# A fused retention and FFN kernel on one core: units of 256 tokens cut in chunks of 64 instead of 128 from block 2 on

## The chip, the cores and the metric

The kernel runs on 1 core of one Trainium2 chip. The metric is the device time of one execution in microseconds (us). The times before are the median of 3 runs. The trace is of one profiled execution, which was timed as well.

In this text PE is TensorE's matmul, PEld its weight load, DVE is VectorE, ACT ScalarE, POOL GpSimd, and SP the engine whose queue issues most of the DMAs.

## The reference

Four sequences (`batch`) with 8 heads of 768 tokens and head size 64 go through a linear recurrence with a decay of its own for each head. Its result, as 3072 tokens of 512 features, goes through two dense layers with a PReLU between.

```python
gamma = 1.0 - 2.0 ** (-5.0 - np.arange(H))
for t in range(S):
    state = gamma * state + einsum('bhd,bhe->bhde', k[:, :, t], v[:, :, t])
    y[:, :, t] = scale * einsum('bhd,bhde->bhe', q[:, :, t], state)
x = y.transpose(0, 2, 1, 3).reshape(B * S, H * D)      # 3072 x 512
h = x @ w_in                                           # 512 -> 2048
out = (maximum(h, 0) + alpha * minimum(h, 0)) @ w_out  # 2048 -> 512
```

## The kernel before, in words

**Tiles, units, blocks.** The recurrence is computed in chunks. A unit `u` is 256 tokens of one sequence: three units to a sequence (`NUS`), twelve in all. A unit has two tiles `w = 2u + g`, 24 in all. Tile `g` holds 256 tokens by 4 heads; a partition holds two neighbouring tokens `a` (token 2p + a), so that its two halves of 64 partitions are the two chunks `c` of 128 tokens. Two units are a block `n` of 512 tokens, six in all, and each block goes through `ffn1` (L540) and `ffn2` (L570).

**The way of a tile.** `load` (L145) has SP issue three DMAs of 256 KB for k, q and v; each partition takes four runs of 512 B. `prep` (L183) scales k and q by powers of the decay into `kdq`, float16 (`scaled`, L190, one instruction each, on POOL from tile 8 on), transposes `kdq` into `kq` so that the head dimension lies on the partitions (from tile 8, `NPE`, on by a DMA transpose from SP at L204, before by PE in `turn`, L230), and casts v into `vx` (L211). The powers are taken relative to the end of a chunk of 128 tokens, so that a state is multiplied by the decay to the 128th at the end of each chunk.

**The products.** Per unit there are four kinds, all on 64 by 64 quadrants of PE, so that four run side by side (`DIAG`, L253):
- scores, k against q within a chunk, masked by DVE into `m2`;
- sums, k against v, the new part of the state;
- inner products, `m2` against `vx`, into `y`;
- carried products, the state at a chunk's start against q, added into `y`; those whose row half equals the chunk are issued first, the others only when a small instruction of DVE or ACT has told that the first are through (`through`, L370), since both write one bank.

The order of the work on each engine is the order of the program: the schedule is written out by hand. In blocks 0 and 1 single tiles go through `visit`, `within` and `finish`. From unit 4 on `both(u_old, u_new)` (L425) does the inner and carried products of one unit and the scores and sums of the next in one call. Before, its order on PE is: the scores of the second new tile, half of them into an `f` bank named `low` and half beside the sums; inner products of both old tiles; carried products of the same half; the scores of the first new tile into the pair of banks `s`; the sums; the carried products of the other half. `masks` (L446) multiplies scores by the causal mask in three parts. DVE then adds the carried state to the sums (L511) and multiplies by the decay (L513) for each of the two chunks. ACT copies `y` to `xT`, the input of `ffn1` (L498).

**The blocks.** The loop at L754 runs `ffn1(n)` and `ffn2(n)` as generators of 64 matmuls each of 512 columns; `tick(gen, m)` issues m of them. `ffn1` sends each of its 16 results through ACT and DVE (L537, L526); `order` names the PSUM bank that each takes. Inside `ffn2(n)` the calls of `both` for the next block are placed: in block 1 after 8 ticks (only scores and sums of unit 4), 28 more and 21 more; in the later blocks after 20 and 33 more. `ahead` (L746) prepares the next tile `w` and then loads tile `w + 4`. So SP's queue holds, in order, the loads of tiles 8 to 11, four stores of block 0's output, then for each tile its transpose followed by the three loads of the tile four on; the stores of each block's output (L602) stand in the same queue.

Of the kernel before, what the change touches and what calls it, by code (L numbers as in the profile page):

```python
# [18 lines left out]
def kernel(  # L19
# [14 lines left out]

    nc = tc.nc
# [24 lines left out]
    for g in range(2):  # L60
        for x in range(2):
            for r in range(2):
                tab_np[64 * r : 64 * r + 64, 32 + 2 * g + x] = g64[4 * g + 2 * r + x] ** 128
    ALT = 48
# [8 lines left out]
    mi_np[:, 256:384] = np.eye(128)  # L73

# [9 lines left out]
    mask = mi[:, 0:256]  # L84
    ident = mi[:, 256:384]
# [59 lines left out]
    def load(w, which="kqv"):  # L145
        u, g, b, c3 = place(w)
        t = staged.setdefault(w, {})
        for nm in which:
            src = {"k": k, "q": q, "v": v}[nm]
            t[nm] = sbp.tile([128, 4, 2 * D], FP, tag=f"{nm}s", bufs=8, name=f"{nm}s{w}")  # L150
            nc.sync.dma_start(  # L151
                out=t[nm],
                in_=src[b, 4 * g : 4 * g + 4, TU * c3 : TU * c3 + TU, :].rearrange(
                    "h (p a) d -> p h (a d)", a=2
                ),
            )
# [26 lines left out]
    def prep(w, opening=False, k_on=None, q_on=None):  # L183
        u, g, b, c3 = place(w)
        t = staged.pop(w)
        kdq = sbp.tile([128, 2, 4, 2, D], F16, tag="kdq", bufs=8, name=f"kdq{w}")
        vx = sbp.tile([128, 4, 2, D], F16, tag="vx", bufs=8, name=f"vx{w}")
        kq = sbp.tile([128, 8, 128], F16, tag="kq", bufs=8, name=f"kq{w}")

        def scaled(eng, kind, src):  # L190
            eng.tensor_tensor(  # L191
                out=kdq[:, kind].rearrange("p z r d -> p r z d"),
                in0=src.rearrange("p (r x) (a d) -> p r (x a) d", a=2, x=2),
                in1=tab[:, 16 * kind + 8 * g : 16 * kind + 8 * g + 8]
                .rearrange("p (r z) -> p r z", r=2)
                .unsqueeze(3)
                .to_broadcast([128, 2, 4, D]),
                op=MULT,
            )

        scaled(k_on or (nc.vector if opening else nc.gpsimd), 0, t["k"])
        scaled(q_on or nc.gpsimd, 1, t["q"])
        if w >= NPE:
            nc.sync.dma_start_transpose(  # L204
                out=kq, in_=kdq.rearrange("p k z r d -> p (k z r d)")
            )
        v_in = t["v"].rearrange("p h (a d) -> p h a d", a=2)
        if opening:
            v_ins[w] = vx, v_in
        else:  # L210
            nc.gpsimd.tensor_copy(out=vx, in_=v_in)  # L211
        prepped[w] = (kdq, kq, vx)
# [86 lines left out]

    def masked(w):  # L300
        kdq, kq, vx, sc = live[w]
        m2 = sbp.tile([128, 4, 2, 128], F16, tag="m2", bufs=4, name="m2")
        nc.vector.tensor_tensor(  # L303
            out=m2.rearrange("p s a i -> p s (a i)"),
            in0=sc.rearrange("p (s n) -> p s n", n=256),
            in1=mask.unsqueeze(1).to_broadcast([128, 4, 256]),
            op=MULT,
        )
        live[w][3] = m2

    def new_state():
        return sbp.tile([128, 4, D], F16, tag="tg", bufs=8, name="tg")

    def state(w, cs=None):
        u, g, b, c3 = place(w)
        decay = tab[:, 32 + 2 * g : 34 + 2 * g].unsqueeze(2).to_broadcast([128, 2, D])
        for c in cs or chunks(w):
# [4 lines left out]
            if 2 * u + c + 1 not in tgs:  # L322
                tgs[2 * u + c + 1] = new_state()
            nc.vector.tensor_tensor(out=tgs[2 * u + c + 1][:, gs], in0=stv, in1=decay, op=MULT)

    def single(g, c, r):
        return slice(256 + 256 * c + 128 * r, 384 + 256 * c + 128 * r)

    def double(g, c, r):
        return slice(512 * c + 256 * g + 128 * r, 512 * c + 256 * g + 128 * r + 128)  # L330

    def carried(w, y, started, same, after=None, at=single):
        u, g, b, c3 = place(w)
        kq = live[w][1]
        for x in range(2):
            for r in range(2):
                c = r if same else 1 - r
                if c3 + c == 0:
                    continue
                ins = nc.tensor.matmul(  # L340
                    out=y[half(x), at(g, c, r)],
# [12 lines left out]
    def inner(w, y, started, at=single):  # L354
        u, g, b, c3 = place(w)
        vx, m2 = live[w][2:4]
        for r in range(2):
            for a in range(2):
                for c, x in DIAG:
                    nc.tensor.matmul(  # L360
                        out=y[half(x), at(g, c, r)],
# [63 lines left out]
    def both(u_old, u_new):  # L425
# [6 lines left out]
        def score(w, at):  # L432
            kq = prepped[w][1]
            for x in range(2):
                for a in range(2):
                    for r, c in DIAG:
                        last = nc.tensor.matmul(  # L437
                            out=at[r][x][half(c), 128 * a : 128 * a + 128],
                            lhsT=kq[half(r), 2 * x + a, half(c)],
                            rhs=kq[half(r), 4 + 2 * x : 6 + 2 * x, half(c)],  # L440
                            start=True,
                            stop=True,
                        )
            return last

        def masks(dst, src):  # L446
            nc.vector.tensor_tensor(  # L447
                out=dst.rearrange("p s a i -> p s (a i)"),
                in0=src.rearrange("p (s n) -> p s n", n=256),
                in1=mask.unsqueeze(1).to_broadcast([128, dst.shape[1], 256]),  # L450
                op=MULT,
            )

        if new:
            u, _, b, c3 = place(new[0])
            cs = chunks(new[0])
            low = ps("low", "fb" if flip["f"] else "fa")
            sums = [ps(f"sums{c}", "pa" if c == 0 else "pb") for c in range(2)]
            beside = [t[:, 256:512] for t in sums]
            there = through(score(new[1], ((low[:, 0:256], low[:, 256:512]), beside)))  # L460
            m2 = [sbp.tile([128, 4, 2, 128], F16, tag="m2", bufs=4, name="m2") for _ in new]
            masks(m2[1][:, 0:2], low)
        if old:
            y = ps("y", "y")
            started = set()
            for w in old:
                inner(w, y, started, double)
            for w in old:
                last = carried(w, y, started, True, None, double)
            done = through(last, nc.scalar)  # L470
        if new:
            sc = ps("sc", "s")
            score(new[0], [[sc[:, 512 * r + 256 * x :][:, 0:256] for x in range(2)] for r in range(2)])
            for w in new:
                kdq, kq, vx = prepped[w]
                for x in range(2):
                    for a in range(2):
                        for c, r in DIAG:
                            if c in cs:
                                at = 128 * (w % 2) + 64 * x  # L480
                                ins = nc.tensor.matmul(  # L481
                                    out=sums[c][half(r), at : at + 64],
                                    lhsT=kdq[half(c), 0, 2 * x + a, r, :],
                                    rhs=vx[half(c), 2 * r + x, a, :],
                                    start=(a == 0),
                                    stop=(a == 1),
                                )
                                if there is not None:
                                    behind(ins, there, "the other row half wrote this bank")
                                    there = None  # L490
        if old:
            for w in old:
                carried(w, y, started, False, done if w == old[0] else None, double)
                live.pop(w)
            n, i = divmod(u_old, 2)
            if i == 0:
                xT[n] = new_x(n)
            nc.scalar.activation(  # L498
                out=xT[n][:, 4 * i : 4 * i + 4].rearrange("p c r (i a) -> p (c r) i a", a=2),
                in_=y.rearrange("p (s a i) -> p s i a", a=2, i=64),  # L500
# [4 lines left out]
        if new:  # L505
            for c in range(2):
                masks(m2[1][:, 2 + c : 3 + c], beside[c])
            for c in cs:
                stv = sums[c][:, 0:256].rearrange("p (z e) -> p z e", e=D)
                if c3 + c > 0:  # L510
                    nc.vector.tensor_tensor(out=stv, in0=tgs[2 * u + c], in1=stv, op=ADD)  # L511
                tgs[2 * u + c + 1] = new_state()
                nc.vector.tensor_tensor(  # L513
                    out=tgs[2 * u + c + 1],
                    in0=stv,
                    in1=tab[:, 32:36].unsqueeze(2).to_broadcast([128, 4, D]),
                    op=MULT,
                )
            masks(m2[0], sc)
            for w, m in zip(new, m2):  # L520
                live[w] = [*prepped.pop(w), m]
# [232 lines left out]
    for n in range(1, NBLK):  # L754
        gen = ffn1(n, "fyfpsYpS" if n > 1 else "spyfSpYf")
# [7 lines left out]
        if n + 1 < NBLK:  # L763
            tick(gen, 8)
            if n == 1:
                both(None, u0)
            ahead()
            ahead()
            tick(gen, 28 if n == 1 else 12)
            both(u0, u0 + 1)  # L770
            tick(gen, 21 if n == 1 else 33)
# [33 lines left out]
```

## Time and profile before

| What | Value |
|---|---|
| Median of 3 runs | 210.43 us (209.54 to 210.77) |
| The profiled execution's own time | 211.09 us |
| Its span, first to last instruction | 209.1 us |
| Mean granted TensorE clock | 0.998 |
| `ffn2` matmuls (L582), 400 | 87.2 us busy |
| `ffn1` matmuls (L557), 392 | 84.8 us busy |
| DMA, mean over the span | 183 GB/s, 38.27 MB |
| Loads of k, q, v | 72, 256 KB each |

The shares of busy time are of the span. Matmuls are pipelined, so their busy times overlap, and the times of the products are better read from the chain of waits, which follows the work that ended last and gives each piece only the time that it added. A DMA share can stand a little over 1, since the time of a packet includes what it overlaps with its neighbours. In a row of the stretches the columns are: the stretch, its length, then for each engine busy time and number of instructions, the granted clock, the DMA share and GB/s.

### The profile page before, as it was taken

Reading aid. Unit: us, or ns where it says so; the run is one execution under the profiler, and the core shown is the slowest. Engines: PE = TensorE matmul, PEld = TensorE weight load, DVE = VectorE, ACT = ScalarE, POOL = GpSimd, SP = SyncE. Lnnn points to the kernel's source line nnn. Section 1 sums busy time; section 2 is a strip of 40 time slices with the busy share of each in tenths; the row PEclk is TensorE's granted clock in tenths of the full one; section 3 lists DMA queues with packets and bytes.
Section 4 is the critical chain, followed back from the end, with each engine's and each line's share of the span. In section 5 each row is a group of like instructions: output and inputs, shape, how many; then the busy total and the mean of one; then the engine's idle time right before and its main releaser. Section 6 shows DMA issues by size and latency. Waiting matters only on the chain.

```text
span 209.1 us, 5197 instructions
## 1 busy us (share of the span) xinstructions
PE 201.5 (96%) x2135; PEld 101.5 (49%) x2135; DVE 123.2 (59%) x209; ACT 97.9 (47%) x166; POOL 72.8 (35%) x97
## 2 busy tenths in 40 slices
PE   7988999999999999999999999999999999999993
PEld 2565445445444555444555444545444544444452
DVE  2583886557588834888373688354888340588000
ACT  2572865174666122666233566233566123665121
POOL 0388798479927664345450054000000000000000
PEclk9999999999999999999999999999999999999999
DMA  6999999999999999799911399111410111100112
GB/s 179 307 286 345 389 389 383 371 312 306 358 254 253 298 252 202 248 233 265 266 71 74 104 235 211 53 56 56 122 31 0 50 53 50 53 0 0 50 55 96
DMA packets 64119, 38.27 MB, mean 183 GB/s; under 512 B 19152, under 2 KB 57568, under 8 KB 64096
## 3 DMA queue, kind: packets, MB, share of 16 engines
q1 hardware_dynamic: 63632, 37.69, 64.6%
q8 instruction: 16, 0.26, 0.5%
q10 hardware_dynamic: 464, 0.25, 0.5%
q14 instruction: 7, 0.06, 0.1%
HBM read 27.45 MB, written 6.29 MB: 161 GB/s over the span
## 4 chain that ended last, share of the span: by engine, by line
PE 88%; SPq 4%; DMA 3%; DVE 1%; ACT 1%; issue 1%; POOL 0%; DVEq 0%; ACTq 0%
PE hps L557 40%; PE ops L582 39%; SPq L151 4%; DMA wi<-in_moe_w_in_dram 3%; PE y L360 2%; PE y L340 2%; PE low L437 1%; PE sums L481 1%; PE sc L437 1%; PE trb L239 1%; DVE m L303 1%; ACT kq L245 0%; PE sc L267 0%; ACT os L596 0%; PE st L292 0%
## 5 line engine op out<-in xcount | busy, mean ns | idle before, releaser
L582 PE MATMUL ops<-wout,gt 128*128 128x512 f16 (+1 forms) x400 | 87.2, 371 | 0.3 <-ACT os L596 0.3
L526 DVE SCALAR_TENSOR_TENSOR gt<-hm,oma,hps 128x512 f16<-128x512 f32 x96 | 71.2, 747 | 26.4 <-ACT hm L537 16.7
L557 PE MATMUL hps<-xT,win 128*128 128x512 f16 (+1 forms) x392 | 84.8, 375 | 0.5 <-POOL win L181 0.5
L537 ACT ACTIVATE hm<-hps 128x512 f32<-128x512 f32 x96 | 57.0, 597 | 24.9 <-PE hps L557 24.5
L557 PEld LDWEIGHTS <-win 128*128 128x128 f16 x392 | 38.0, 98 | 45.3 <-POOL win L181 0.7
L582 PEld LDWEIGHTS <-gt 128*128 128x128 f16 x400 | 37.9, 98 | 41.4 <-issue 0.6
L596 ACT ACTIVATE os<-ops 128x512 f32<-128x512 f32 (+2 forms) x25 | 14.2, 576 | 46.6 <-PE ops L582 46.6
L191 POOL TENSOR_TENSOR kdq<-ks,tab 128x512 f16<-128x512 f32 x19 | 19.8, 1042 | 38.6 <-DMA ks<-in_k_dram 30.5
L191 POOL TENSOR_TENSOR kdq<-qs,tab 128x512 f16<-128x512 f32 x22 | 23.2, 1054 | 9.4 <-DMA ks<-in_k_dram 7.8
L447 DVE TENSOR_TENSOR m<-low,mi 128x512 f16<-128x512 f32 x8 | 5.5, 686 | 24.8 <-issue 24.0
L245 ACT ACTIVATE kq<-trb 128x512 f16<-128x512 f16 (+1 forms) x12 | 8.6, 736 | 10.7 <-PE trb L239 10.6
L211 POOL CAST vx<-vs 128x512 f16<-128x512 f32 x16 | 9.8, 610 | 3.5 <-PE y L360 3.0
L181 POOL CAST win<-wi 128x512 f16<-128x512 f32 x16 | 9.8, 613 | 2.8 <-DMA wi<-in_moe_w_in_dram 2.3
L181 POOL CAST wout<-wo 128x512 f16<-128x512 f32 x16 | 9.6, 613 | 3.3 <-DMA wo<-in_moe_w_out_dram 3.1
L303 DVE TENSOR_TENSOR m<-sc,mi 128x1024 f16<-128x1024 f32 x8 | 9.8, 1222 | 0.8 <-PE sc L267 0.4
L498 ACT ACTIVATE xT<-y 128x1024 f16<-128x1024 f32 x8 | 8.2, 1023 | 3.3 <-PE y L340 3.3
L447 DVE TENSOR_TENSOR m<-sc,mi 128x1024 f16<-128x1024 f32 x8 | 9.7, 1214 | 0.0
L340 PE MATMUL y<-kq,tg 64*64 64x128 f16 x160 | 8.5, 224 | 0.5 <-ACT word L374 0.4
L360 PE MATMUL y<-m,vx 64*64 64x128 f16 x384 | 8.3, 218 | 0.2 <-DVE m L303 0.2
L219 PE MATMUL trb<-ones 128*128 128x512 f16 (+1 forms) x21 | 6.5, 434 | 1.5 <-DVE word L624 1.4
L374 ACT ACTIVATE word<-word 1x1 f32<-1x1 f32 x11 | 2.2, 201 | 12.1 <-PE y L340 12.1
L600 DVE COPY os<-ops 128x128 f32<-128x128 f32 x1 | 0.3, 291 | 12.8 <-ACT os L596 12.8
(39 smaller groups left out, 99.5 us busy)
## 6 DMA issues: line engine op xcount, KB each, us to landing
ks<-in_k_dram SPq DMA_DIRECT2D x24, 256.0 KB, 4.6
qs<-in_q_dram SPq DMA_DIRECT2D x24, 256.0 KB, 4.7
vs<-in_v_dram SPq DMA_DIRECT2D x24, 256.0 KB, 4.8
out_dram<-os SPq DMA_DIRECT2D x23, 256.0 KB, 2.2
wi<-in_moe_w_in_dram SPq DMA_DIRECT2D x16, 256.0 KB, 6.1
wo<-in_moe_w_out_dram SPq DMA_DIRECT2D x16, 256.0 KB, 5.3
kq<-kdq SPq DMA_TRANSPOSE x16, 4.9
mi<-mi_const ACTq DMA_DIRECT2D x1, 128.0 KB, 3.5
```

What stands on the lines that cost most here:

```text
L181: nc.gpsimd.tensor_copy(out=dst, in_=t)
L191: eng.tensor_tensor(out=kdq[:, kind].rearrange("p z r d -> p r z d"), in0=src.rearrange("p (r x) (a d) -> p r (x a) d", a=2, x=2), in1=tab ...
L211: nc.gpsimd.tensor_copy(out=vx, in_=v_in)
L303: nc.vector.tensor_tensor(out=m2.rearrange("p s a i -> p s (a i)"), in0=sc.rearrange("p (s n) -> p s n", n=256), in1=mask.unsqueeze(1).to_ ...
L340: ins = nc.tensor.matmul(out=y[half(x), at(g, c, r)], lhsT=tgs[2 * u + c][half(r), 2 * g + x, :], rhs=kq[half(r), 4 + 2 * x : 6 + 2 * x, h ...
L360: nc.tensor.matmul(out=y[half(x), at(g, c, r)], lhsT=vx[half(c), 2 * r + x, a, :], rhs=m2[half(c), 2 * r + x, a, :], start=(c, x) not in s ...
L447: nc.vector.tensor_tensor(out=dst.rearrange("p s a i -> p s (a i)"), in0=src.rearrange("p (s n) -> p s n", n=256), in1=mask.unsqueeze(1).t ...
L526: nc.vector.scalar_tensor_tensor(out=gt[:, ft, lo:hi], in0=hm, scalar=oma_sb[:, ft : ft + 1], in1=hps, op0=MULT, op1=ADD,)
L537: nc.scalar.activation(out=hm, in_=hps, func=RELU, bias=0.0, scale=-1.0)
L557: nc.tensor.matmul(out=hpss[ft][:, 128 * lo : 128 * hi], lhsT=w_in_all[:, hp, 128 * ft : 128 * ft + 128], rhs=xT[n].rearrange("p (g t) r i ...
L582: nc.tensor.matmul(out=opss[tq], lhsT=gt[:, ft, 128 * tq : 128 * tq + 128], rhs=w_out_all[:, ft, at], start=(ft == 0), stop=(ft == NFT - 1),)
L596: nc.scalar.activation(out=os_sb, in_=opss[tq][:, cut], func=COPY, bias=0.0, scale=1.0)
```

## The change

From unit 4 (block 2's first, tile 8) on a tile is 128 tokens by all 8 heads, one token to a partition, and its two chunks are 64 tokens each. A unit of 256 tokens is again two tiles, now one after the other in time.

- `load`: a partition takes eight runs of 256 B, one of each head, where it took four of 512 B.
- `scaled`: two instructions of half the size each, with tables of their own.
- Scores, inner products and carried products have 64 columns instead of 128. A unit has 32 scores (32 before), 32 inner products (32), 32 sums (32), 32 carried products (16). In a sequence's last unit the sums of the last chunk are left out as before.
- All scores go into the pair `s`, and one mask instruction of 1024 columns serves the unit. The parts in `low` and beside the sums go, and with them one tell by DVE.
- The state is stepped four times per unit. The powers stay relative to the end of 128 tokens, so between the two chunks of a tile the sums are only added, and the decay is multiplied in at the end of a tile.
- In `both` the old unit's inner and carried products come first, then the scores and sums of the new one, then the other carried products.
- Buffers: `m2` 3 instead of 4, states 12 instead of 8. The bank order of `ffn1` changes from block 2 on.
- Places: in `ffn2` both `ahead` calls come first. In block 1 `both` comes after 2 ticks, 24 and 26 more; in the later blocks after 14 and 28 more.

Shortened to its core:

```diff
 def load
+            else:
+                at = TU * c3 + 128 * g
+                nc.sync.dma_start(
+                    out=t[nm].rearrange("p a (b d) -> p (a b) d", b=2),
+                    in_=src[b, :, at : at + 128, :].rearrange("h p d -> p h d"),
+                )
...
 def both
+        if old:
+            for w in old:
+                                out=out_of(y, w, x, c, g, r),
+                                lhsT=vx[half(c), 2 * g + r, x, :],
+                                rhs=m2[half(c), at : at + 64],
+            for w in old:
+                last = carry(w, y, True)
+            done = through(last, nc.scalar)
         if new:
+            js = range(3 if c3 == NUS - 1 else 4)
             sc = ps("sc", "s")
+            for w in new:
+                            out=sc[half(c), at : at + 64],
+                            lhsT=kq[half(r), z, half(c)],
+                            rhs=kq[half(r), 4 + z, half(c)],
+            for w in new:
+                                out=sums[c][half(r), at : at + 64],
+                                lhsT=kdq[half(c), 0, z, r, :],
+                                rhs=vx[half(c), 2 * (z // 2) + r, z % 2, :],
         if old:
+                carry(w, y, False, done if w == old[0] else None)
...
+            for j in js:
+                t, c = divmod(j, 2)
+                    nc.vector.tensor_tensor(out=stv if last else to, in0=tgs[4 * u + j], in1=stv, op=ADD)
+                if last:
+                    nc.vector.tensor_tensor(out=to, in0=stv, in1=tab[:, 32:36]..., op=MULT)
...
-        gen = ffn1(n, "fyfpsYpS" if n > 1 else "spyfSpYf")
+        gen = ffn1(n, "fspyfSpY" if n > 1 else "spyfSpYf")
...
-            tick(gen, 8)
+            ahead()
+            ahead()
+            tick(gen, 2 if n == 1 else 14)
             if n == 1:
                 both(None, u0)
-            ahead()
-            ahead()
-            tick(gen, 28 if n == 1 else 12)
+                tick(gen, 24)
             both(u0, u0 + 1)
-            tick(gen, 21 if n == 1 else 33)
+            tick(gen, 26 if n == 1 else 28)
             both(u0 + 1, u0 + 2 if 2 * u0 + 4 < NW else None)
```

## Prediction, before the change was run

> **What bounds the kernel now.** I read the page's shares first, then the chain of waits around the attention steps of the FFN blocks, then the queue that loads q, k and v.
>
> ```profile
> PE 201.5 (96%) x2135; PEld 101.5 (49%) x2135; DVE 123.2 (59%) x209; ACT 97.9 (47%) x166; POOL 72.8 (35%) x97
> ...
> DMA  6999999999999999799911399111410111100112
> ```
>
> TensorE bounds it: PE is busy 96% of the span, VectorE and ScalarE about half. Each digit of the DMA row is 5.2 us, and it is full up to 84 us and again until 104 us: in the first half the DMA engines have nothing to spare.
>
> The chain of waits through one call of `both` (units 8 and 9), start, length, what:
>
> ```profile
> 134.66 0.17 PE low L437
> ...
> 135.01 0.45 PE y L360 x32
> 135.46 0.11 PE y L340 x8
> 135.57 0.22 PE sc L437 x16
> 135.79 0.25 PE sums L481 x32
> 136.04 0.14 PE y L340 x7
> 136.18 0.97 PE ops L582 x4
> ```
>
> The call holds PE from 134.66 to 136.18, 1.52 us, without a wait. The reader should see two prices. Products of 128 columns: 32 in 0.45 us, 16 in 0.22, so 56 ns for each round of four (one per quadrant). Products of 64 columns (`sums`): 32 in 0.25 us, 31 ns a round, with as many weight loads. The first 16 take 0.35 us (134.66 to 135.01), 0.13 more than the later 16: the price of entering.
>
> The loads, on SP's queue, and the last weights of tile 13 (the timeline of SP, its transposes' landing, the timeline of PEld):
>
> ```profile
> 42.16 1.47 SPq L151 DMA_DIRECT2D ks<-in_k_dram  x1
> ...
> 51.80 0.68 SPq L151 DMA_DIRECT2D vs<-in_v_dram  x1
> 52.58 0.64 SPq L602 DMA_DIRECT2D out_dram<-os  x1
> ```
>
> ```profile
> DMA to landing us min/median/max: 6.1/6.1/6.1
> ```
>
> ```profile
> 82.34 0.26 PEld L437 LDWEIGHTS <-kq 64*64 64x64 f16 x16 [0.42 <-DMA kq<-kdq]
> ```
>
> From 42.16 SP issues the 12 loads of tiles 8 to 11; the next kind of issue comes at 52.58, so they go at 0.868 us each (10.42 / 12). The transpose of tile 13, issued at 75.84, lands 6.1 us later, at 81.94, and PE uses it at 82.34. So in block 1 a wait of the data path ends only just ahead of PE: 0.4 us of slack.
>
> **What the change does on PE.** A full call now issues 32 inner products, 16 carried, 32 scores, 32 sums and 16 carried, all of 64 columns: 32 rounds at 31 ns, 1.00 us, with 0.13 for entering and about 0.06 for leaving (136.04 to 136.18 less two rounds): 1.19 us. The seven full calls of the chain take 1.50 to 1.58, mean 1.54: **0.35 us saved, seven times, 2.45 us.** The call with nothing old took 1.09 (69.01 to 70.10), 0.2 of it a wait for a VectorE tell that goes; it becomes 0.13 + 0.25 + 0.25 + 0.05 = 0.68, saving 0.41. The call with nothing new took 1.36 (174.33 to 175.69); its ScalarE tell is still uncovered, and the products in front shrink by 0.2. Sum: **3.06 us off PE**, 1.11 of it in block 1. Bounds for a row that trace has only for `sums`: if scores and inner products of 64 columns cost a round 56 ns, a full call is 32 x 0.056 + 0.19 = 1.98 and the change loses 0.44 on each of seven; below 31 ns no row goes. I take 31: the shape is the same 64x64.
>
> **Other engines.** VectorE per unit: before, masks of 0.69 + 2 x 0.42 + 1.21 and four state steps of 0.42, 4.4 us; after, one mask of 1.21 and six state steps, 3.7 us. It has 5.3 us (24 ticks) or more until the next call; nothing gained or lost. POOL's scaling is cut in two instructions of half the size; its fixed part is at most the 0.10 us of its smallest MEMSETs, so 0.2 us per tile. Tile 13 was ready on POOL at 68.1 and its transpose issued at 75.84, so 7 us cover it. ScalarE's tell runs 0.36 us behind the carried products; the 64 products between them take 0.50 us (0.47 before), still a cover. The freed `f` bank, the three `m2`, the twelve states and the new bank order put no one on the path: `s` is used again 2.6 us or more after its mask may start.
>
> **The loads.** From tile 8 on, a load of 256 KB is 1024 packets of 256 B, where it was 512 of 512 B. No row shows such a load. Three rows bound it (share and GB/s of the DMA in stretches where one kind runs: opening loads, weight pieces, and two transposes with one store):
>
> ```profile
> 1.50:9.50 8.00, 7.53 (x51) 3.71 (x52) 3.29 (x5) 3.29 (x6) 1.04 (x1) 1.00 0.97 283
> 21.00:25.00 4.00, 4.00 (x20) 1.73 (x19) 3.48 (x6) 3.45 (x7) 2.70 (x5) 1.00 1.05 400
> 148.00:154.00 6.00, 6.00 (x30) 2.69 (x29) 4.88 (x7) 4.14 (x8) 0.00 (x0) 1.00 0.52 131
> ```
>
> 256 KB in 2 KB packets (128 of them) take 262144 / 400e3 = 0.655 us; in 512 packets 0.868. The 384 further packets cost 0.55 ns each, so 512 more cost **0.28 us: 1.15 us a load.** The transposes move as many packets of 256 B: 0.52 x 6 = 3.12 us of engine time, less 0.655 for the store, halved: 1.23, which is +0.36. Ends: nothing (+0; packets cost by bytes alone; the same bytes in more packets give no reason for a gain) and a packet of 256 B as dear as one of 512 (+0.87). I take +0.28, next to the transposes. As likely I read 0.36 down to half of my value, 0.14, since packets overlap (the DMA share of 57 to 84 us is 1.18) and part of it may hide there.
>
> The Trainium skill (DMA: Bandwidth & Descriptors, Why small descriptors are slow) gives each packet 3 fixed cycles beside one per 32 B: 22 cycles for two of 256 B against 19 for one of 512. By that estimate a load costs 16% more, +0.14, and the sum below is +1.4 us instead of +5.2; the rows above show a larger fixed part.
>
> **Where that cost falls.** The loads are one queue with the transposes, in the order tiles 8 to 11, then transpose w, load w + 4. Ahead of the transpose of tile 9 stand 15 new loads, of tile 11 21, of tile 13 27. The engines are full from 42 to 57 us; from 57 to 84 the pauses are at the transposes and remain. So the landings (before: 59.90 + 5.2 = 65.1; 67.61 + 5.9 = 73.5; 81.94) move to 69.3, 79.4 and 89.5.
>
> PE wants them earlier than before, since block 1 now has its calls after 2, 24 and 26 ticks, not 8, 28 and 21. A tick is 0.221 us (67.28 to 85.61 less the calls, by 64). From ffn2's start at 67.28: first call 67.72, scores of tile 9 at 67.98, end 68.40; second call 73.70, scores of tile 11 behind inner and carried products at 74.33; third call 80.63, scores of tile 13 at 81.26. The waits: 1.3 at tile 9; 79.4 - 75.6 = 3.7 at tile 11; 89.5 - 86.3 = 3.2 at tile 13: **8.2 us of PE waiting where there was none.** All three together are simply 89.5 - 81.26.
>
> Later tiles have room: tile 17 landed at 103.8, its call came at 112.4, and its four tiles lose 3.4 us; 18 to 23 land 9 us or more ahead.
>
> **Sum.** -3.06 + 8.24 = +5.2 us. The profiled execution has a span of 209.1 and a time of 211.09, 0.3% over the median of 210.43. On the span 214.3; on the median **215.6 us**. With 0.14 per load tile 13 lands at 85.7, PE waits 4.5, and it is +1.4 (211.8); with 0.36 at 91.7, 10.4 and +7.3 (217.8).
>
> **Rivals.**
> 1. Packets cost by bytes, the loads keep their time. Tile 13 lands at 81.94, PE waits 0.7, the result is -2.4: **208.0, faster.** The rows of 512 B packets stand at 283 to 309 GB/s against 400 for 2 KB, which speaks against it; that the queue also pauses at transposes, where a slower load could hide, speaks a little for it. It decides at a wait of 3.06 us, that is tile 13 at 84.3, or 0.088 us per load.
> 2. A packet of 256 B takes as long as one of 512: +0.87 x 27 = 23.5, a wait of 24.2, **231.5**. The row of the transposes (1.23 us for 1024) speaks against it. The Trainium skill (DMA: Bandwidth & Descriptors, Specifications) puts the line rate at 512 B and more, with a read-modify-write below; by that rule this rival would be the outcome. That chance is small, as transposes of 256 B packets do not show it.
> 3. The small products don't shrink, 56 ns a round. The 3.06 gained becomes some 3 lost, part of it under the waits: **about 220**. The `sums` row speaks against it.
>
> **Chances.** Forecast 58% (211.8 to 217.8), rival 1 27%, rival 2 8%, rival 3 7%. The range leaves out rivals 2 and 3: 207.8 to 218.5; by the forecast alone 211.8 to 217.8. Half a per cent, 1.05 us, is about what a measurement of this kernel can tell. Faster is rival 1 without its upper edge, 24%; same 9% (the edges of rival 1 and of the forecast); slower 67%.
>
> **What would show it.** Right: PEld waits for `kq` in block 1 for 1 to 4 us at each of three calls, ffn1 of block 2 starts near 92 us instead of 85.6, full calls last about 1.2 us, and loads issue at 1.1 to 1.2 us each from 42 us on. Wrong: no such wait (rival 1), or calls still of 1.5 us (rival 3). The weakest number is the packet price, since 27 of them add up ahead of one product.

## The result, and the profile after

The changed kernel takes 216.03 us (median of 4 runs, 215.74 to 217.12), beside 210.06 us (4 runs) for the kernel before: a ratio of 1.0267, 95% interval 1.0213 to 1.0320. By the ratio it is slower by about 5.6 us; 215.6 us was forecast. The profiled execution has a span of 214.3 us, 5.2 more than before. In the experiments below the kernel before ran beside each on the same chip, with medians of 211.3 to 211.4 us, so ratios are compared. The ratios leave out executions more than 1.5% above the fastest of their kernel; where the profiled execution is one of these, the text calls it the longest, and only the places of its waits and its clock are used.

The page of the changed kernel, rows of PE, of the clock granted to it and of the DMA engines, 5.36 us to a digit:

```profile
PE 200.7 (94%) x2287; PEld 99.9 (47%) x2287; DVE 120.2 (56%) x195; ACT 97.7 (46%) x166; POOL 77.3 (36%) x129
...
PEclk9999999999999996999999999999999999999999
DMA  6999999999999999999997179611240012100112
```

PE is busy for 0.8 us less than before in a span that is 5.2 longer, there is one dip of its clock, and the DMA row, full up to 84 us before, is full up to 112.

The chain of waits through the call of `both` for units 8 and 9, the one shown of before:

```profile
139.69 0.37 PE y L490 x32
140.06 0.13 PE y L468 x14
140.19 0.27 PE sc L511 x30
140.46 0.29 PE sums L525 x32
140.75 0.16 PE y L468 x15
140.91 1.19 PE ops L634 x5
```

It lasts 1.22 us (139.69 to 140.91) where it lasted 1.52: the products are cheaper, as intended. The loss is in block 1. SP's queue, with the transposes of tiles 11 (75.33) and 13 (84.45), the time from issue to landing of tile 13's, and PEld, where the bracket gives the idle time before the row and what ended it:

```profile
42.59 1.47 SPq L166 DMA_DIRECT2D ks<-in_k_dram  x1
...
55.96 1.39 SPq L166 DMA_DIRECT2D vs<-in_v_dram  x1
57.43 2.56 SPq L654 DMA_DIRECT2D out_dram<-os  x4
...
75.33 1.70 SPq L230 DMA_TRANSPOSE kq<-kdq  x1
...
84.45 2.16 SPq L230 DMA_TRANSPOSE kq<-kdq  x1
```

```profile
DMA to landing us min/median/max: 4.1/4.1/4.1
```

```profile
68.82 0.21 PEld L511 LDWEIGHTS <-kq 64*64 64x64 f16 x16 [0.84 <-DMA kq<-kdq]
...
80.57 0.29 PEld L511 LDWEIGHTS <-kq 64*64 64x64 f16 x16 [5.25 <-DMA kq<-kdq]
...
88.77 0.39 PEld L511 LDWEIGHTS <-kq 64*64 64x64 f16 x32
```

The 12 loads of tiles 8 to 11 take 14.84 us (42.59 to 57.43), 1.24 us each, where they took 0.87. PE waits for tile 9, then 5.1 us for tile 11 (of the 5.25, PE's own row counts 5.14), and not for tile 13, which lands at 88.55, 0.2 us before the row that loads the weights of tiles 12 and 13 begins. `ffn1` of block 2 starts 6.8 us later; its rows in the chain of waits, before and after:

```profile
85.61 13.81 PE hps L557 x64
```

```profile
92.42 3.67 PE hps L609 x17
```

One thing was not in the forecast. The stretches behind the long wait (stretch, length, busy times, granted clock, DMA share, GB/s):

```profile
80.50:82.00 1.50, 1.43 (x58) 1.09 (x59) 0.94 (x1) 0.30 (x1) 0.54 (x1) 0.50 1.27 286
82.00:84.00 2.00, 2.00 (x7) 0.77 (x6) 1.89 (x5) 0.72 (x1) 2.00 (x5) 0.55 1.09 245
84.00:86.00 2.00, 2.00 (x11) 0.94 (x10) 0.00 (x0) 0.60 (x1) 0.61 (x2) 1.00 1.19 269
```

After standing idle for 5.1 us PE is granted half its clock for some 3 us. The chain of waits gives the 26 ticks behind that call 6.80 us (81.64 to 88.44), where at 0.221 a tick they would take 5.74.

### The profile page after: what moved, and what is told of

Same layout as the page of the kernel before. It is cut to its first block, busy times and chain, and to the rows that moved or that the text cites. A ratio compares the mean times of both kernels' runs of the same rounds, so it can differ in the third digit from the quotient of the medians.

```text
span 214.3 us, 5523 instructions
## 1 busy us (share of the span) xinstructions
PE 200.7 (94%) x2287; PEld 99.9 (47%) x2287; DVE 120.2 (56%) x195; ACT 97.7 (46%) x166; POOL 77.3 (36%) x129
## 4 chain that ended last, share of the span: by engine, by line
PE 69%; DMA 17%; SPq 7%; POOL 2%; DVE 1%; issue 1%; ACT 1%; POOLq 0%; DVEq 0%; ACTq 0%
PE ops L634 32%; PE hps L609 31%; DMA wo<-in_moe_w_out_dram 5%; SPq L158 4%; DMA wi<-in_moe_w_in_dram 4%; DMA ks<-in_k_dram 3%; DMA qs<-in_q_dram 3%; SPq L189 2%; DMA kq<-kdq 2%; PE y L490 1%; POOL wout L194 1%; PE y L468 1%; PE sums L525 1%; PE sc L511 1%; SPq L230 1%
## 5 line engine op out<-in xcount | busy, mean ns | idle before, releaser
L634 PE MATMUL ops<-wout,gt 128*128 128x512 f16 (+1 forms) x400 | 88.2, 374 | 0.4 <-ACT os L648 0.3
L207 POOL TENSOR_TENSOR kdq<-ks,tab 128x256 f16<-128x256 f32 x32 | 18.9, 613 | 39.3 <-PE hps L609 16.7
L207 POOL TENSOR_TENSOR kdq<-qs,tab 128x256 f16<-128x256 f32 x32 | 18.9, 613 | 1.7 <-DMA qs<-in_q_dram 1.7
L539 ACT ACTIVATE xT<-y 128x1024 f16<-128x1024 f32 x8 | 8.2, 1024 | 9.8 <-PE y L468 9.8
L511 PE MATMUL sc<-kq 64*64 64x64 f16 x256 | 4.2, 199 | 5.9 <-DMA kq<-kdq 5.9
L217 POOL TENSOR_TENSOR kdq<-qs,tab 128x512 f16<-128x512 f32 x6 | 6.3, 1043 | 9.3 <-DMA ks<-in_k_dram 7.5
L426 ACT ACTIVATE xT<-y 128x512 f16<-128x512 f32 x8 | 4.8, 597 | 5.7 <-PE y L364 5.7
```

Of the source, the lines that this page charges most:

```text
L207: eng.tensor_tensor(out=kdq[:, kind, 2 * i : 2 * i + 2].rearrange("p x r d -> p r x d"), in0=src[:, 2 * i : 2 * i + 2].rearrange("p r (x d ...
L634: nc.tensor.matmul(out=opss[tq], lhsT=gt[:, ft, 128 * tq : 128 * tq + 128], rhs=w_out_all[:, ft, at], start=(ft == 0), stop=(ft == NFT - 1),)
```

## The experiments

**Theory 1**, the forecast's: the loads in packets of 256 B take longer, they stand in one queue ahead of the transposes, and transposes that are due land late. **Theory 2**: block 1's calls merely stand too early, or the new order of the products costs the time. **Theory 3**, on the way: the DMA engines' total work is the limit, in whatever order.

### The old loads under the new products, and the new loads under the old

The changed kernel with the old loads:

```diff
-            if w < NPE:
+            if True:
                 nc.sync.dma_start(out=t[nm],
                     in_=src[b, 4 * g : 4 * g + 4, TU * c3 : TU * c3 + TU, :].rearrange(
                         "h (p a) d -> p h (a d)", a=2))
```

> The changed kernel, but from tile 8 on the loads take the old pattern (512 packets of 512 B, 256 tokens by 4 heads), so the numbers that reach the products are other tokens' and heads'; all instructions and sizes behind them are the changed kernel's. If the 256 B packets are the cause (theory 1), the 12 loads of tiles 8 to 11 go at about 0.87 us each again, the transpose of tile 13 lands near 82, PE waits under 1 us in block 1, and the time is about 208 (before 210.1, less 3 of products, plus 0.7 of waits). If the new places of the calls or the order of the products are the cause (theory 2), it stays at 215 to 216.

Measured: 208.36 us (4 runs), ratio to before 0.9883 (0.9821 to 0.9944). PEld's rows in block 1:

```profile
66.83 0.33 PEld L511 LDWEIGHTS <-kq 64*64 64x64 f16 x32 [0.42 <-DMA kq<-kdq]
...
72.76 0.33 PEld L490 LDWEIGHTS <-vx 64*64 64x64 f16 x32 [0.42 <-issue]
...
73.16 0.39 PEld L511 LDWEIGHTS <-kq 64*64 64x64 f16 x32
...
80.17 0.39 PEld L511 LDWEIGHTS <-kq 64*64 64x64 f16 x32
```

The 0.42 us is what PEld shows at the start of every call, with or without a DMA to wait for. All three calls run through at the new places, and the 12 loads take 0.89 us each (41.11 to 51.83). Places, order and POOL's split scaling are those of the changed kernel, so theory 2 falls, and the change without its loads makes the kernel faster by 1.2%.

The kernel before with the new loads:

```diff
+            if w < NPE:
                 nc.sync.dma_start(out=t[nm], ...)
+            else:
+                at = TU * c3 + 128 * g
+                nc.sync.dma_start(
+                    out=t[nm].rearrange("p a (b d) -> p (a b) d", b=2),
+                    in_=src[b, :, at : at + 128, :].rearrange("h p d -> p h d"))
```

> The kernel before, but from tile 8 on the loads take the new pattern (1024 packets of 256 B, 128 tokens by 8 heads), so other tokens and heads reach the products; the products and the places of the calls are those of before. Theory 1: the transpose of tile 11 lands near 80.5 and that of tile 13 near 88.5, against needs at 76.2 and 82.4, so PE waits 4 and then 2 us in block 1, with a lower clock behind the longer one: 216 to 218. Theory 2 (places or order of the products): 210.

Measured: 218.17 us (4 runs), ratio 1.0329 (1.0257 to 1.0400). PEld's rows:

```profile
75.52 0.26 PEld L444 LDWEIGHTS <-kq 64*64 64x64 f16 x16 [1.38 <-DMA kq<-kdq]
86.14 0.40 PEld L444 LDWEIGHTS <-kq 64*64 64x64 f16 x16 [4.89 <-DMA kq<-kdq]
```

The loads alone make the old kernel slower by 3.3%, and the waits stand at the same tiles, 11 and 13. I had expected 4 and then 2 us; it was 1.0 and 4.5 (less the 0.42). In this execution the loads of tile 8 began at 40.19, 2.4 us earlier than in the changed kernel's (42.59). Tile 13 landed at 86.15, which is as long behind that start, 46.0 us; tile 11, at 75.5, was 2.7 us quicker than there. The expectation left out that the start moves, and how late the queue is at a single tile varies.

The four kernels together: the new loads cost 3.3% under the old products and 3.9% under the new ones (1.0267 / 0.9883).

### Block 1's calls at the old places

```diff
-            tick(gen, 2 if n == 1 else 14)
+            tick(gen, 8 if n == 1 else 14)
...
-                tick(gen, 24)
+                tick(gen, 28)
...
-            tick(gen, 26 if n == 1 else 28)
+            tick(gen, 21 if n == 1 else 28)
```

> The changed kernel with block 1's calls at the old places (after 8 ticks, 28 and 21 more). Theory 1: the landing of tile 13's transpose near 88.5 sets the end of block 1, and only the 12 ticks that stood behind the last call shrink to 7; the wait for tile 11 is 2.6 us shorter and no second long wait follows: about 214.5 to 215.5. Theory 2 (the calls merely stand too early): the waits go and the time is 207 to 208.

Measured: 215.38 us (4 runs), ratio 1.0190 (1.0116 to 1.0265), which overlaps the changed kernel's interval. In the profiled execution, the longest of the four, the wait for tile 11 shrinks to 0.9 us and one of 5.0 us stands at tile 13:

```profile
79.10 0.21 PEld L511 LDWEIGHTS <-kq 64*64 64x64 f16 x16 [0.86 <-DMA kq<-kdq]
...
90.39 0.30 PEld L511 LDWEIGHTS <-kq 64*64 64x64 f16 x16 [4.99 <-DMA kq<-kdq]
```

The time is the one expected, but I had expected no second long wait. Moving the calls moves the wait; in this execution the landing of the last transpose sets the end. Theory 2's 207 to 208 us is excluded.

### The queue in another order

First block 1 alone: the transposes of tiles 8 to 11, loads 12 and 13, transposes 12 and 13, loads 14 to 17.

```diff
             prep(w)
-            if w + WB < NW:
+            if w in (11, 13):
+                for i in range(w + 1, w + 3) if w == 11 else range(14, 18):
+                    load(i)
+            elif w + WB < NW and w > 13:
                 load(w + WB)
```

> The changed kernel with SP's queue reordered in block 1: the transposes of tiles 8 to 11 come before the loads of 12 and 13, those of 12 and 13 before the loads of 14 to 17. Bytes, packets and products are the same. Theory 1 (the price of the loads falls on PE only because loads stand ahead of transposes that are due): tile 9 lands near 66, tile 11 near 70, tile 13 near 81 to 82, PE waits at most 1 us, and the time is 207 to 208.5, below both kernels. If the DMA engines' total work in block 1 is the limit, whatever its order (theory 3), the waits stay and the time is 213 or more.

Measured: 213.82 us, the median of 6 runs from 209.81 to 215.54, too far apart for an interval. Neither theory had this outcome: the time is theory 3's, but the waits are not. In the profiled execution, the longest, all waits of block 1 are gone, and a long one stands in block 2, at tile 17:

```profile
115.20 0.30 PEld L511 LDWEIGHTS <-kq 64*64 64x64 f16 x16 [4.71 <-DMA kq<-kdq]
```

The gain was given back a block later. PE is now early, and in block 2 again three loads stand ahead of each transpose. So the same was done there:

```diff
+            elif w == 17:
+                for i in range(18, 22):
+                    load(i)
-            elif w + WB < NW and w > 13:
+            elif w + WB < NW and w > 17:
                 load(w + WB)
```

> The changed kernel with SP's queue reordered in blocks 1 and 2: transposes of tiles 8 to 11, loads 12 and 13, transposes 12 and 13, loads 14 to 17, then in block 2 transposes 14 to 17 ahead of loads 18 to 21. In the run with block 1 alone reordered, the waits of block 1 went and one of 4.7 us appeared at tile 17 in block 2. If that wait is the same mechanism moved on (loads in front of a transpose that is due), it goes: tile 17 lands before 108, no wait for kq is over 1 us anywhere, and the time is 206.5 to 208, 2 to 3 us under the kernel before. If the DMA engines' total work is the limit, a wait of 3 us or more stays in block 2 or 3 and the time is 210 or more.

Measured: 207.37 us (6 runs, 207.23 to 209.27), ratio 0.9854 (0.9814 to 0.9894): 1.5% faster than the kernel before and, by the two ratios, 4% faster than the changed one, with the same bytes, packets and products. No wait for a `kq` that a DMA brings is left. SP's queue, and the chain of waits of block 1:

```profile
58.11 5.49 SPq L230 DMA_TRANSPOSE kq<-kdq  x4
```

```profile
66.79 0.38 PE sc L511 x32
67.17 0.27 PE sums L525 x32
67.44 5.29 PE ops L634 x24
72.72 0.38 PE y L490 x32
...
79.71 0.38 PE y L490 x32
...
80.99 2.70 PE ops L634 x12
```

Four transposes go out in a row, and the chain passes through the three calls without a DMA in it. Theory 3 falls as well: the engines have the time for these loads, if none stands in front of a transpose that is due. This is the version that beats both.

The control puts the same order into the kernel before:

> The kernel before with the same order of SP's queue as a control. It has no wait for kq to lose, so if the gain of the reordered changed kernel comes from its smaller products, this one stays within 0.5% of the kernel before (209.5 to 211). If the order itself is worth something, it is faster by 1 us or more.

Measured: 210.24 us (10 runs, nine from 209.56 to 211.85 and one of 262.86), ratio 0.9971 (0.9935 to 1.0006). The order alone is worth nothing that shows; it only lets the smaller products count.

### The clock after the wait

```diff
                 kq = prepped[w][1]
+                if w == 11:
+                    for _ in range(48):
+                        nc.tensor.matmul(out=sc[:, 256:512], lhsT=ones[:, 0:128],
+                                         rhs=ones[:, 0:256], start=True, stop=True)
```

> The changed kernel with 48 idle products of 256 columns (5.2 us of PE work) put where PE waits for tile 11's transpose; their result is overwritten. If the lower granted clock of 80.5 to 84 us in the changed kernel comes from PE having stood idle for 5 us, the granted clock stays at 1.0, the 26 ticks behind that call take 5.7 us instead of 6.8, and the time is 1.0 to 1.5 us under the changed kernel's (214.5 to 215). If the clock falls for another reason, it stays at 216.

Measured: 215.39 us (4 runs), ratio 1.0191 (1.0134 to 1.0248). That is 0.8% below the changed kernel's 1.0267, about the gain that was expected, but the two intervals overlap, so it is not shown that the time follows. The stretches that were at half clock, and PEld's row of tile 13, in the profiled execution, the longest of the four:

```profile
80.00:82.00 2.00, 2.00 (x70) 1.65 (x68) 0.34 (x1) 0.00 (x0) 0.61 (x1) 1.00 0.94 211
82.00:84.00 2.00, 2.00 (x10) 0.91 (x11) 1.93 (x4) 1.60 (x2) 1.17 (x3) 1.00 1.66 264
```

```profile
91.23 0.21 PEld L516 LDWEIGHTS <-kq 64*64 64x64 f16 x16 [2.97 <-DMA kq<-kdq]
```

The clock stays at 1.00, so the half clock came of the idle time. In this execution PE then waits 3.0 us for tile 13, mostly because its transpose landed late, at 91.2, where it landed at 88.55 in the changed kernel.

What the slow clock cost the changed kernel can be estimated from its own rows. The scores of tile 12 start at 88.95 there, those of tile 13 some 0.15 us later. Without the slow clock PE would have come to the latter about 1.4 us earlier, at 87.7, and waited until tile 13 landed at 88.55. If that landing stays where it is, about 0.9 of the 1.4 us only stands in place of this wait, and about 0.5 us is lost.

### The price of a packet by itself

The kernel before, with 18 loads more behind the stores of block 4, where the DMA engines are quiet:

```diff
+        if n + 1 == NBLK:
+            for run in (512, 256, 128):
+                for i in range(6):
+                    t, src = ...
+                    nc.sync.dma_start(out=t, in_=src)
         gen = ffn1(...)
```

> The kernel before with 18 loads more in the quiet DMA stretch of block 5 (near 179 us), into buffers that nobody reads: six of 512 packets of 512 B, six of 1024 packets of 256 B, six of 1024 packets of 128 B (half the bytes). From a fixed part of 0.55 to 0.65 ns for each packet and the rest by bytes: 0.87 to 0.92, 1.15 to 1.25 and about 0.85 to 0.95 us a load. If a packet of 256 B is as dear as one of 512: 0.87, 1.74 and 1.74. If packets cost by bytes alone: 0.87, 0.87 and 0.43. The time of the kernel stays as before.

The three kinds (512, 256 and 128 B), each in a stretch where it runs alone; the last column is GB/s:

```profile
183.80:185.40 1.60, 1.60 (x9) 0.76 (x8) 1.36 (x3) 1.07 (x3) 0.00 (x0) 1.00 1.07 320
189.00:192.00 3.00, 3.00 (x15) 1.36 (x14) 2.54 (x5) 1.94 (x5) 0.00 (x0) 1.00 1.07 243
195.00:197.50 2.50, 2.50 (x13) 1.17 (x12) 0.00 (x0) 0.60 (x1) 0.00 (x0) 1.00 1.01 157
```

262144 B at 320 and 243 GB/s are 0.82 and 1.08 us a load; 131072 B at 157 are 0.83. All three are a little under what was expected. So 512 packets more of the same bytes cost 0.26 us (0.21 against the 0.87 us of block 1's loads before; the 512 B stretch is only 1.6 us long), and 1024 packets of half the bytes cost as much as 512 of all: a fixed part for each packet and the rest by bytes. The loads of 256 B also take their addresses in another order (8 heads of 128 tokens, not 4 of 256); no run of 512 B packets has the new order. But from the two smaller kinds, which share it, half the bytes are 0.25 us and 1024 packets 0.58 us; by these 512 packets of all the bytes would take 0.79 us, close to the 0.82 measured in the old order. The kernel's time is that of before, ratio 1.0004 (0.9968 to 1.0041).

## Why the prediction was right, point by point

**The price of a load.** Forecast +0.28 us, from the slope between packets of 2 KB and of 512 B; alone it is +0.26, in the queue ahead of block 1's transposes +0.37 (1.24 against 0.87). Why it is more there is not settled. Of the rivals, packets by bytes alone (+0) and packets as dear as the larger ones (+0.87) are both excluded. The Trainium skill (DMA: Bandwidth & Descriptors, Why small descriptors are slow) gives, as an estimate from its fixed cycles, +16%; measured are +32% alone and +42% in the queue. The Trainium skill (same page, Specifications) puts the line rate at 512 B and more; here packets of 256 B are slower than those of 512 B, 243 against 320 GB/s, but far from twice as slow.

**The landings.** Tile 9 forecast 69.3, measured 68.8 (64.70 + 4.1); tile 11 79.4 and 80.5 (75.33 + 5.2); tile 13 89.5 and 88.55 (84.45 + 4.1). That they agree within 1.1 us is in part luck: the transposes were issued 0.6 to 1.8 us later than the forecast implies (59.90 + 4.2, 67.61 + 5.9 and 75.84 + 7.6) and landed 0.7 to 2.0 us sooner after their issue than in the kernel before.

**The waits.** Forecast 1.3 + 3.7 + 3.2 = 8.2 us. Measured 0.7 + 5.1 + 0, which is 5.9 in PE's rows (0.73 and 5.14). This term is mis-sized by 2.3: tile 11 was later than forecast, so tile 13 was already there when PE came, and PE came later still because of the clock. The sign named beforehand, 1 to 4 us at each of three calls, came only in part; `ffn1` of block 2 near 92 us, calls of about 1.2 us and slower loads (1.24 us each, a little above the 1.1 to 1.2 named) did come.

**The clock, a term that was missing.** 1.06 us over the 26 ticks, and about 0.4 within the call before them (from the wait's end to the ticks 1.07 us, 80.57 to 81.64, where the calls without a wait need 0.6 to 0.7).

**The products.** Forecast -3.06. In blocks 2 to 5 the five full calls and the last take 7.39 us where they took 9.05: -1.66 against -1.95 forecast. A full call takes 1.17 to 1.34, where 1.19 was forecast; scores and sums go at 0.27 to 0.32 for 32 (once 0.41) instead of 0.25. The 0.06 us for leaving does not follow from its row: 0.14 less two rounds of 56 ns is 0.03. Block 1 without waits, read from the reordered kernel: 0.65, 1.27 and 1.28 against 1.09, 1.52 and 1.58, so -0.99 against -1.11. Together -2.65. Rival 3, that they don't shrink, is excluded.

**POOL.** Its fixed part was put at 0.10 us at most; half an instruction takes 0.61 us where a whole one takes 1.04, so it is about 0.18. Nothing here hangs on it: tile 13 was scaled by 73.7 and its transpose was issued at 84.45.

**The sum.** -2.65 + 5.9 + 1.06 + 0.4 = +4.7, against +5.2 of the span. PEld's brackets for the two waits, 0.84 and 5.25, would give 6.1 instead of 5.9; I can't assign the remaining 0.3. Forecast was -3.06 + 8.24 = +5.2. The mechanism, its block and the last landing were right, and the sum came out almost exactly. The exactness is luck: a wait too large by 2.3 us stands against a clock term of 1.4 that was missing and 0.4 of the products' saving that did not come. The first two are not independent, though: the forecast's waits add up to the last landing less PE's need of 81.26, and with the measured landing that is 88.55 - 81.26 = 7.3 us, which is what the measured waits and the clock add up to (5.9 + 1.4). So tile 13's landing nearly set the end, as forecast, with the clock in the place of the third wait.

**Later tiles.** That they would have room held for the changed kernel, but only because PE was already late: once block 1's waits were gone, tile 17 was next. I had called its 8.6 us of slack in the kernel before enough, and did not work it out for the case without waits.

## What to carry to other kernels

A change of layout that halves the contiguous run of a load is a change of the DMA queue: price the packets, count the loads ahead of each transfer that is due, and compare landings with needs, tile by tile. Where a saving on the busiest engine makes it earlier, ask which transfer is then due first, and again after that one is mended. Before a better layout is given up for its loads, try their order: transfers that somebody waits for go ahead of those that are only being fetched.

## What the runs showed of the hardware that was not expected

PE idle for 5.1 us (changed kernel), 4.9 us (old places), 4.6 us (block 1 reordered) and 4.4 us (old kernel with the new loads), by PE's own rows, was each time followed by 3 to 6 us at a granted clock of about 0.50; a wait of 2.9 us (in the kernel with the filling products) was followed by 1.00. This agrees with the Trainium skill (TensorE: Matmul & The Clock Gate, Part 1: The HAM clock gate), which puts the clock at half after an idle window of about 3.4 us. So a wait between two dense stretches can cost more than its length: in the changed kernel the work behind a wait of 5.1 us took 1.4 us longer, although there, by the estimate above, most of that stood in place of another wait.
